# Another order of token tiles and of loads in the last step of a convolution (state-space layer beside a feed-forward layer)

## The chip, the core and the metric

The kernel runs on one core of one Trainium2 chip. The core has a matrix engine (TensorE, PE in the profile), a vector engine (VectorE, DVE), a scalar engine (ScalarE, ACT), GpSimd (POOL) and SyncE (SP), which here only issues transfers. All transfers between HBM and the core's memory (SBUF) run on the core's 16 DMA engines, whichever queue issues them. TensorE writes its products to PSUM, from where VectorE or ScalarE fetch them.

The metric is the device time of one execution in microseconds (us). Lower is better.

## The reference: what is computed

```python
x = A_u                                   # 1 x 2048 tokens x 576
xn = layernorm(x)
K[d, l] = Re sum_n C[d, n] * exp(dt[d] * A[d, n] * l) * dt[d] * B[d, n]
conv = irfft(rfft(xn padded) * rfft(K padded))[:2048] + xn * Dskip
ffn = silu(xn @ w1) @ w2                  # 576 -> 4608 -> 576
out = x + conv + ffn
```

Everything is float32. The convolution over 2048 tokens is done in the frequency domain, as a chain of small matrix products. The last of them turns an intermediate `d2` (4096 x 576, in HBM) back into tokens.

## The kernel before

**Tokens.** The 2048 tokens are 16 tiles of 128, numbered j = 0 to 15. Each has a running sum of 128 x 576, started with x, to which the feed-forward part and the convolution are added.

**The feed-forward part is the main line.** `ffn` goes over `blocks`: two halves of the tokens (`half` 0: j 0 to 7, `half` 1: j 8 to 15), 9 chunks c of four 128-wide pieces of the hidden layer, and two blocks b of four token tiles. In a block (half, c, b), `up(blk, t)` makes piece t of the hidden layer (14 matmuls of 128 x 512, on TensorE, lines L291 to L293), which ScalarE turns into `gf` and `gh` and VectorE into `gl` (L299 to L301). `down(blk, jj)` multiplies by w2 for one token tile: two half-rows of 288 columns, 12 matmuls each (L316), into one of three PSUM buffers `ps2`, and VectorE adds each half to `acc[j]` (L320). The order in a block is one up of the next block, four downs, then three ups of the next block (`u0, d0, d1, d2, d3, u1, u2, u3`). Each is a step; there are 288 steps (`2 * NCH * 2 * (FT + 4)`). Block (1,7,0) has steps 261 to 268, (1,7,1) has 269 to 276, (1,8,0) has 277 to 284 and the last, (1,8,1), 285 to 288.

The weights of a chunk are loaded and split into a high and a low part while the previous chunk runs. `load_w1(…, t)` brings two pieces of w1 in three transfers (L246 to L248; 512, 64 and 64 KB) into `w1r`, `split_w1` makes `w1h` on ScalarE (L259) and `w1l` on VectorE (L261) for each. `load_w2` and `split_w2` do it for one piece of w2 (L269, 288 KB; L278 and L280). For the last chunk all loads are traced behind step 261, the split of the second `w1r` pair behind step 269, with the table `after` of L379. The second `w1r` pair and the last two `w2r` tiles of that chunk lie in the pool `yp`, which takes over the memory of the frequency-domain stage.

**The convolution is the side line.** `side` is a generator that yields due times, as shares of the 288 steps; `weave` (L32) runs it on whenever its due time has been reached. At its end comes `tail`, the last convolution step for tiles 0 to 7, whose sums were put away in HBM (`dr0`) after half 0.

- `conv_load(j)` (L776) brings `ys`, the 256 rows of `d2` for tile j, in two transfers of 288 KB from SyncE's queue (L780). There are `AHEAD + 2` = 8 buffers.
- `add_conv(j, dst)` (L783) is the product: 8 small matmuls on TensorE (16 in the profile, L793) into two of the three PSUM buffers `pss`, and two adds on VectorE into `dst` (L799). Its first matmul stands behind the last matmul of the feed-forward part that was traced before it.
- `load_r0(j)` (L735) brings the sums of tiles j and j + 1 back, 576 KB.
- `store` (L172) writes a finished pair of tiles, for tiles 0 to 7 from GpSimd's queue.

`tail` places its loads 0.0045 apart from 0.895 on, that is from step 258: `ys0`, `r0` 0, `ys1`, `ys2`, `r0` 2, `ys3`, `ys4`, `r0` 4, `ys5`, `ys6`, `r0` 6, `ys7`. The products of tiles 0 to 7 (`last`) have their due times 0.005 apart from 0.922 on: behind steps 266, 267, 269, 270, 272, 273, 275 and 276. With product j of tiles 2 to 7 goes the load of tile j + 6. The products of tiles 8 to 15 stand in `down` in the last chunk (L307), ahead of that tile's matmuls, with the loads of tiles 14 and 15. `d2` must be complete before the first `ys` load, because every tile needs rows of all 32 frequency steps.

**How the order on the chip comes about.** Before the program runs, a planner turns the traced instructions into one fixed queue for each engine (`schedule_with_timeline_sim`, L940): by its own timeline it gives an instruction its place when its operands are there; of several that are ready, what was traced earlier goes first, and what is traced under `tc.high_priority()` (L298, L319) before that. `behind(ins)` holds instructions behind `ins` in its queue. On the chip each engine runs its queue in that order and waits where an operand is late. SyncE's queue works the same way; each of its transfers also waits for the one eight before it to land.

Of the kernel before, what the change touches and what calls it, by code (L numbers as in the profile page):

```python
# [11 lines left out]
F32 = mybir.dt.float32  # L12
# [6 lines left out]
P = 128  # L19
# [4 lines left out]
NJ = 16  # L24
NKT = 4
HD = D // 2
# [16 lines left out]
def kernel(  # L43
# [89 lines left out]
    pins = {}  # L133

    def behind(ins):
        return tc.issue_after(ins) if ins is not None else nullcontext()
# [24 lines left out]
    def load_x(j, pool, tag, engines):  # L161

        t = pool.tile([P, 2, D], F32, tag=tag, name=f"{tag}{j}")
        for ps, v, eng in quarters(xv, engines):
            eng.dma_start(t[ps], v[:, j:j + 2])
        pairs[j] = t
        return t[:, 0, :], t[:, 1, :]

    def store(t, j, engines):

        for ps, v, eng in quarters(ov, engines):
            eng.dma_start(v[:, j:j + 2] if len(t.shape) > 2 else v[:, j], t[ps])  # L172
# [26 lines left out]
    def phase0(p0, js):  # L199
        j0 = js[0]  # L200
        xs = load_x(j0, accp, "acc", (nc.sync, nc.scalar) if j0 < 4 else (nc.sync,))
        acc.update(zip(js, xs))
        if j0:
            normed(p0, js, xs)
        else:
            for j, xj in zip(js, xs):
                normed(p0, (j,), (xj,))
# [23 lines left out]
    def ffn():  # L231
# [71 lines left out]
        def down(blk, jj):  # L303
            half, c, b = blk
            j = 8 * half + 4 * b + jj
            js = slice(jj * P, (jj + 1) * P)
            if half == 1 and c == NCH - 1:  # L307
                conv_load(j + AHEAD)
                add_conv(j, acc[j])
            for h in range(2):  # L310
                hs = slice(h * HD, (h + 1) * HD)
                po = ps2.tile([P, 512], F32, tag="ps2", name="po")
                n = 0
                for t in range(FT):
                    for g, w in ((0, 0), (0, 1), (1, 0)):
                        pins["pe"] = nc.tensor.matmul(po[:, :HD], G[blk, t][g][:, js], W2[half, c, t][w][:, hs],  # L316
                                                      start=n == 0, stop=n == 3 * FT - 1).ins
                        n += 1
                with tc.high_priority():  # L319
                    nc.vector.tensor_add(acc[j][:, hs], po[:, :HD], acc[j][:, hs])  # L320
            if half == 0 and c == NCH - 1:
                rows = slice(j * P, (j + 1) * P)
                nc.sync.dma_start(dr0[rows, :], acc[j])
                if j % 2:
                    acc[7 + j], acc[8 + j] = load_x(7 + j, accp, "acc", (nc.sync,))
# [398 lines left out]
            nc.gpsimd.dma_start(d2.rearrange("(p k) d -> k p d", k=32)[k], yo)  # L724
            yield 1 + (k + 1) / 32

    AHEAD = 6

    def tail():

        r0s = {}

        def load_r0(j):
            r0s[j] = yp.tile([P, 2, D], F32, tag="r0", name="r0", bufs=4)
            nc.sync.dma_start(r0s[j], dr0[j * P:(j + 2) * P, :].rearrange("(i p) d -> p i d", p=P))  # L735

        def last(j):
            conv_load(j + AHEAD, 8)
            add_conv(j, r0s[j - j % 2][:, j % 2, :])
            if j % 2:  # L740
                store(r0s[j - 1], j - 1, (nc.gpsimd,))

        steps, at = [], tail_at[0]
        for j in range(8):
            for f in (conv_load, load_r0)[:2 - j % 2]:
                steps.append((at, f, j))
                at += tail_at[1]
        steps += [(tail_at[2] + j * tail_at[3], last, j) for j in range(8)]
        for at, f, j in sorted(steps, key=lambda v: v[0]):
            yield at  # L750
            with behind(pins["load"]):
                f(j)

    yss = {}

# [17 lines left out]
                nc.tensor.matmul(dst, st, mv[:, hs], start=n == 0, stop=n == 3 * len(terms) - 1)  # L773
                n += 1

    def conv_load(j, first=0):  # L776
        if first <= j < NJ:
            yss[j] = yp.tile([P, 4, HD], F32, tag="ys", name="ys", bufs=AHEAD + 2)
            for h in range(2):
                nc.sync.dma_start(yss[j][64 * h:64 * h + 64],  # L780
                                  d2[j * 256:(j + 1) * 256, h * HD:(h + 1) * HD].rearrange("(q r) d -> r q d", q=4))

    def add_conv(j, dst):  # L783

        ys = yss.pop(j)
        py = [pss.tile([P, 512], F32, tag="pss", name="py") for _ in range(2)]
        first = pins["pe"]
        for n in range(8):
            q1, q2, h = n // 4, n // 2 % 2, 1 - n % 2
            o = 64 * q1 + 32 * q2  # L790
            rows = slice(64 * h, 64 * h + 64)
            with tc.high_priority() if n else nullcontext(), behind(first):
                mm = nc.tensor.matmul(py[h][o:o + 32, :HD], s4[rows], ys[rows, 2 * q2 + q1],  # L793
                                      start=True, stop=True, tile_position=(64 * h, o), skip_group_check=True)
            if n == 0:
                first = mm.ins
        for h in range(2):
            hs = slice(h * HD, (h + 1) * HD)
            nc.vector.tensor_add(dst[:, hs], py[h][:, :HD], dst[:, hs])  # L799

    def gate_of(i):

        return (FT + i * 2 * FT + 1) / (2 * NCH * 2 * 2 * FT)

    def side():
        nonlocal s4, kl, yp, pa, tail_at
        marks = (0.13, 0.597, 0.823)
        tail_at = (0.895, 0.0045, 0.922, 0.005)
        with tc.tile_pool(name="pa", bufs=4) as pa:
            for js in ((0, 1), (2, 3), (4, 5), (6, 7)):  # L810
                with behind(pins["xt3"] if js[0] > 2 else None):
                    phase0(pa, js)
                pins[f"xt{js[1]}"], pins[f"xt{js[1]}s"] = pins["xt_v"], pins["xt_s"]
                if js[0] == 2:
                    yield 0
            yield 0
        with tc.tile_pool(name="kf", bufs=1) as kfp:
            for n in ("f", "phi"):
                kf[n] = kfp.tile([P, D], F32, name=n + "T")
            with tc.tile_pool(name="nat", bufs=1) as nat, tc.tile_pool(name="pb", bufs=1) as pb:  # L820
                nt = natural(nat)
                def late(j):

                    xs = load_x(j, pb, "xj", (nc.sync,))
                    yield
                    with behind(pins["gl"]):
                        normed(pb, (j, j + 1), xs)
                    yield

                tiles = chain.from_iterable(late(j) for j in range(8, NJ, 2))  # L830
                for at, todo in ((0.0, nt), (0.0, tiles), (0.004, tiles), (0.005, tiles), (gate_of(0), nt), (0.026, tiles), (0.028, tiles), (0.036, tiles), (0.038, tiles), (gate_of(1), nt), (0.06, tiles), (gate_of(2), nt), (0.09, nt)):
                    yield at
                    with behind(pins["gl"] if at else None):
                        next(todo, None)
            with behind(pins["sd"]):
                nc.gpsimd.dma_start(f1, cf1)
            nc.sync.dma_start(vt, cv)
            with tc.tile_pool(name="up", bufs=1) as up:
                sp = spread(up)
                for n, at in enumerate(kgen()):  # L840
                    if n > 1:
                        next(sp, None)
                    yield marks[0] + at * (marks[1] - marks[0])
                for _ in sp:
                    pass
        s4p = ctx.enter_context(tc.tile_pool(name="s4p", bufs=1))
        s4 = s4p.tile([P, 32], F32, name="s4")
        nc.gpsimd.dma_start(s4, cs4)

        with tc.tile_pool(name="kl", bufs=2) as kl:  # L850
            for at in spectral():
                yield marks[1] + (at - 1) * (marks[2] - marks[1])
        yp = ctx.enter_context(tc.tile_pool(name="yp", bufs=3))
        yield from tail()

    sd = side()
    next(sd)
    fg = ffn()
# [85 lines left out]
```

## Time and profile before

| | us |
|---|---|
| three runs | 1133.81, 1135.52, 1135.73 (median 1135.52) |
| the profiled execution | 1134.37 |
| its span, first to last instruction | 1132.6 |
| mean granted TensorE clock | 0.997 |
| TensorE from 1030 to 1050, 1050 to 1070, 1070 to 1090: busy | 17.77, 17.92, 18.54 of 20 each |
| TensorE from 1090 to 1120: busy | 30.00 of 30 |
| transfers from 1029 to 1094 | 15.48 MB, 238 GB/s |
| end of the last matmul | 1128.3 |

In a profile page PE is TensorE's matmuls and PEld its weight loads; L316 is line 316 of the kernel, and `po<-w2h,gh` names the tile that is written and those that are read. `x16` counts instructions merged in a line of the timeline: first the start, then the time from first to last of them, and in brackets how long the engine had been idle and who ended that. A row of the waits gives the total in us, how many times, and the longest. A row of the table by stretches has the stretch, its length, the busy time of each engine with the number of instructions (PE, PEld, DVE, ACT, POOL), the granted clock, the share of the 16 DMA engines that was busy (sums above 1 occur, since packets overlap) and GB/s.

### The profile page before, as it was taken

What the parts mean: (1) busy time and instruction counts of PE and PEld (TensorE: products, weight loads), DVE (VectorE), ACT (ScalarE), POOL (GpSimd) and SP (SyncE); (2) the same over time, 40 slices, a digit from 0 to 9 for tenths busy, and PEclk for the clock granted to TensorE, in tenths of its full rate; (3) what the DMA queues carried; (4) which work ended last, traced back from release to release, by engine and by line L of the source; (5) the groups of instructions that cost most, each with busy time, mean ns of one, the idle gap of its engine ahead of it and who ended that gap; (6) DMA issues with size and microseconds to landing.
All of it is one profiled execution on the core that took longest, in us unless ns stands there. A gap on an engine that the chain in (4) does not pass through costs nothing.

```text
span 1132.6 us, 22870 instructions
## 1 busy us (share of the span) xinstructions
PE 1108.6 (98%) x9144; PEld 998.8 (88%) x9144; DVE 916.8 (81%) x1545; ACT 709.3 (63%) x1229; POOL 73.0 (6%) x130
## 2 busy tenths in 40 slices
PE   6999999999999999999999999999999999999898
PEld 5988889898898898889989999999999999997776
DVE  6798799999999899999999737777778787773433
ACT  4565366677767676676766636787777787772211
POOL 1100100000000000011000000000000000001110
PEclk9999999999999999999999999999999999999999
DMA  9546431425252415265743263554555454426971
GB/s 277 152 121 168 122 83 60 107 81 128 71 116 84 115 60 129 70 152 168 193 143 93 67 165 115 150 154 134 160 152 159 127 158 141 132 89 170 248 179 56
DMA packets 174971, 148.56 MB, mean 131 GB/s; under 512 B 110944, under 2 KB 141680, under 8 KB 174736
## 3 DMA queue, kind: packets, MB, share of 16 engines
q1 hardware_dynamic: 164768, 112.07, 37.8%
q0 software_dynamic: 9712, 34.14, 9.4%
q8 instruction: 72, 1.18, 0.5%
q10 hardware_dynamic: 384, 0.89, 0.3%
q14 instruction: 35, 0.29, 0.1%
HBM read 102.53 MB, written 44.61 MB: 130 GB/s over the span
## 4 chain that ended last, share of the span: by engine, by line
PE 77%; DMA 7%; DVE 7%; issue 4%; SPq 2%; ACT 2%; POOL 0%; ACTq 0%; DVEq 0%; POOLq 0%
PE po L316 33%; PE ph L291 27%; DMA ys<-d 3%; PE kp L641 3%; PE ph L293 2%; PE ph L292 2%; PE pu L773 2%; PE pk L773 2%; PE pb L773 2%; PE z L656 2%; PE pu L154 1%; SPq L228 1%; DVE st L181 1%; DMA xj<-in_A_u_dram 1%; DVE gl L301 1%
## 5 line engine op out<-in xcount | busy, mean ns | idle before, releaser
L316 PE MATMUL po<-w2h,gh 128*128 128x288 f32 x1152 | 338.6, 298 | 1.0 <-ACT w2h L278 0.9
L316 PE MATMUL po<-w2l,gh 128*128 128x288 f32 x1152 | 339.0, 295 | 0.0
L316 PE MATMUL po<-w2h,gl 128*128 128x288 f32 x1152 | 337.1, 296 | 2.0 <-DVE gl L301 1.8
L316 PEld LDWEIGHTS po<-w2h,gh 128*128 128x128 f32 x1152 | 215.9, 188 | 11.6 <-issue 3.7
L316 PEld LDWEIGHTS po<-w2h,gl 128*128 128x128 f32 x1152 | 216.1, 188 | 4.8 <-DVE gl L301 2.8
L316 PEld LDWEIGHTS po<-w2l,gh 128*128 128x128 f32 x1152 | 217.0, 188 | 3.7
L299 ACT ACTIVATE gf<-ph 128x512 f32<-128x512 f32 (+1 forms) x148 | 86.5, 585 | 126.1 <-PE ph L293 109.3
L320 DVE TENSOR_TENSOR acc<-po,acc 128x288 f32<-128x288 f32 x288 | 127.1, 454 | 46.9 <-PE po L316 45.0
L291 PE MATMUL ph<-xh,w1h 128*128 128x512 f32 (+1 forms) x592 | 163.3, 391 | 1.4 <-ACT xh L124 0.7
L291 PE MATMUL ph<-xl,w1h 128*128 128x512 f32 (+1 forms) x592 | 162.9, 389 | 0.0
L291 PE MATMUL ph<-xh,w1l 128*128 128x512 f32 (+1 forms) x592 | 162.5, 387 | 0.3 <-DVE w1l L261 0.3
L301 DVE TENSOR_TENSOR gl<-gf,gh 128x512 fp32r<-128x512 f32 (+1 forms) x148 | 99.4, 674 | 39.8 <-ACT gh L300 39.0
L291 PEld LDWEIGHTS ph<-xl,w1h 128*128 128x128 f32 x592 | 109.5, 191 | 20.7
L291 PEld LDWEIGHTS ph<-xh,w1l 128*128 128x128 f32 x592 | 108.2, 189 | 21.0 <-DVE w1l L261 0.7
L291 PEld LDWEIGHTS ph<-xh,w1h 128*128 128x128 f32 x592 | 105.7, 190 | 20.3 <-issue 2.3
L300 ACT CAST gh<-gf 128x512 fp32r<-128x512 f32 (+1 forms) x148 | 89.8, 609 | 14.2 <-PE po L316 11.2
L278 ACT CAST w2h<-w2r 128x576 fp32r<-128x576 f32 x72 | 46.9, 672 | 44.8 <-PE po L316 27.9
L600 ACT ACTIVATE c<-th 128x1040 f32<-128x1040 f32 x36 | 38.7, 1074 | 49.3 <-DVE th L599 49.3
L598 ACT ACTIVATE c<-th,magic 128x1040 f32<-128x1040 f32 x36 | 42.0, 1168 | 33.2 <-DVE th L584 17.2
L261 DVE TENSOR_TENSOR w1l<-w1r,w1h 128x640 fp32r<-128x640 f32 x72 | 57.1, 822 | 0.2
L292 PE MATMUL ph<-x,w1h 128*128 128x512 f32 (+1 forms) x148 | 57.1, 386 | 0.0
L293 PE MATMUL ph<-x,w1l 128*128 128x512 f32 (+1 forms) x148 | 57.1, 386 | 0.0
(182 smaller groups left out, 1829.2 us busy)
## 6 DMA issues: line engine op xcount, KB each, us to landing
w2r<-in_B_w_dram SPq DMA_DIRECT2D x72, 288.0 KB, 3.3
w1r<-in_B_w_dram SPq DMA_DIRECT2D x35, 512.0 KB, 4.1
d1u<-u POOLq DMA_DIRECT2D x32, 288.0 KB, 2.7
d1k<-stage SPq DMA_DIRECT2D x18, 512.0 KB, 7.4
ur<-d1u SPq DMA_DIRECT2D x32, 288.0 KB, 4.1
kr<-d1k SPq DMA_DIRECT2D x32, 288.0 KB, 2.8
d<-yo POOLq DMA_DIRECT2D x32, 288.0 KB, 3.6
ys<-d SPq DMA_DIRECT2D x32, 288.0 KB, 12.4
```

The costliest lines, as they stand in the source:

```text
L261: pins["w1l"] = nc.vector.tensor_sub(l1, src, h1).ins
L278: pins["w2h"] = nc.scalar.copy(h2, r2).ins
L291: nc.tensor.matmul(ph, w[:, kt, :], v[:, kt, a:e], start=n + kt == 0, stop=False)
L292: nc.tensor.matmul(ph, h1[:, 4, :], x4[:, a:e], start=False, stop=False)
L293: pins["pe"] = nc.tensor.matmul(ph, l1[:, 4, :], x4[:, a:e], start=False, stop=True).ins
L299: nc.scalar.activation(gf, ph, AF.Silu)
L300: pins["gh"] = nc.scalar.copy(gh, gf).ins
L301: pins["gl"] = nc.vector.tensor_sub(gl, gf, gh).ins
L316: pins["pe"] = nc.tensor.matmul(po[:, :HD], G[blk, t][g][:, js], W2[half, c, t][w][:, hs], start=n == 0, stop=n == 3 * FT - 1).ins
L320: nc.vector.tensor_add(acc[j][:, hs], po[:, :HD], acc[j][:, hs])
L598: nc.scalar.activation(c65, th, AF.Identity, bias=magic)
L773: nc.tensor.matmul(dst, st, mv[:, hs], start=n == 0, stop=n == 3 * len(terms) - 1)
```

## The change

The product order becomes 0 to 3, 8 to 11, 4 to 7, 12 to 15, and the loads follow the same order through one iterator. The first eight `ys` loads and two of the `r0` loads are traced together at 0.897, step 259, ahead of the weights of the last chunk (step 261). Each product, after its own matmuls and adds, calls for the next load. Products 0 to 3 have due times that put them behind steps 269 to 272, products 4 to 7 behind 278, 279, 280 and 282; `r0` 4 and `r0` 6 are loaded after products 1 and 2. The products of tiles 8 to 15 stay in `down`, so that in block (1,8,0) the order on TensorE is to be 8, down 0, 4, 9, down 1, 5, 10, down 2, 6, 11, down 3, an up, 7. The number of buffers stays 8.

```diff
             if half == 1 and c == NCH - 1:
-                conv_load(j + AHEAD)
                 add_conv(j, acc[j])
+                conv_load()
...
-    AHEAD = 6
+
+    order = iter((0, 1, 2, 3, 8, 9, 10, 11, 4, 5, 6, 7, 12, 13, 14, 15))
...
         def last(j):
-            conv_load(j + AHEAD, 8)
             add_conv(j, r0s[j - j % 2][:, j % 2, :])
+            conv_load()
             if j % 2:
                 store(r0s[j - 1], j - 1, (nc.gpsimd,))
 
-        steps, at = [], tail_at[0]
+        yield tail_at[0]
+        with behind(pins["load"]):
+            for j in (0, None, 2, None, None, None, None, None):
+                conv_load()
+                if j is not None:
+                    load_r0(j)
         for j in range(8):
-            for f in (conv_load, load_r0)[:2 - j % 2]:
-                steps.append((at, f, j))
-                at += tail_at[1]
-        steps += [(tail_at[2] + j * tail_at[3], last, j) for j in range(8)]
-        for at, f, j in sorted(steps, key=lambda v: v[0]):
-            yield at
-            with behind(pins["load"]):
-                f(j)
+            if j in (2, 3):
+                load_r0(j * 2)
+            yield tail_at[1 + j // 4] + j % 4 * tail_at[3]
+            last(j)
...
-    def conv_load(j, first=0):
-        if first <= j < NJ:
-            yss[j] = yp.tile([P, 4, HD], F32, tag="ys", name="ys", bufs=AHEAD + 2)
+    def conv_load():
+
+        j = next(order, None)
+        if j is not None:
+            yss[j] = yp.tile([P, 4, HD], F32, tag="ys", name="ys", bufs=8)
...
-        tail_at = (0.895, 0.0045, 0.922, 0.005)
+        tail_at = (0.897, 0.932, 0.965, 0.0036)
```

## The prediction

> **What bounds the kernel now.** I read the page first, then the waits, then the timelines of TensorE, of SyncE's queue and of VectorE over the last 110 us. The page:
>
> ```profile
> PE 1108.6 (98%) x9144; PEld 998.8 (88%) x9144; DVE 916.8 (81%) x1545; ACT 709.3 (63%) x1229; POOL 73.0 (6%) x130
> ys<-d SPq DMA_DIRECT2D x32, 288.0 KB, 12.4
> ```
>
> TensorE is busy for 98% of the span, so a change can win only where it idles. A `ys` half takes 12.4 us from issue to landing; a lone load of 288 KB takes 2.8 us (`kr<-d1k`, 288.0 KB, 2.8, on the same list): transfers queue up. The waits of TensorE from 1020 us to the end are one line, and its timeline shows where:
>
> ```profile
> PE py L793 <- DMA ys<-d: 5.8, 4, 2.1
> ```
>
> ```profile
> 1036.91 0.71 PE L793 MATMUL py<-ys,s 64*32 64x288 f32 x16
> ...
> 1039.97 0.69 PE L793 MATMUL py<-ys,s 64*32 64x288 f32 x8 [0.99 <-DMA ys<-d]
> ...
> 1048.90 0.84 PE L793 MATMUL py<-ys,s 64*32 64x288 f32 x16 [1.23 <-DMA ys<-d]
> ...
> 1055.18 0.84 PE L793 MATMUL py<-ys,s 64*32 64x288 f32 x16 [2.08 <-DMA ys<-d]
> ...
> 1056.46 0.44 PE L316 MATMUL po<-w2h,gh 128*128 128x288 f32 x1
> ```
>
> Products 1, 2, 3 and 7 wait for their `ys` tile, 5.8 us together. After the longest gap 14 matmuls run at a pace of 0.24 us instead of 0.13 (0.44 us each instead of 0.29). SyncE's queue shows in which order the transfers stand, and the table by stretches what the DMA engines can do:
>
> ```profile
> 1029.41 1.28 SPq L780 DMA_DIRECT2D ys<-d  x2
> 1030.74 0.60 SPq L735 DMA_DIRECT2D r<-dr  x1
> 1031.38 1.24 SPq L780 DMA_DIRECT2D ys<-d  x2
> 1032.66 0.61 SPq L246 DMA_DIRECT2D w1r<-in_B_w_dram  x1
> ...
> 1034.38 0.60 SPq L248 DMA_DIRECT2D w1r<-in_B_w_dram  x1
> 1035.02 1.06 SPq L269 DMA_DIRECT2D w2r<-in_B_w_dram  x2
> 1037.52 1.59 SPq L780 DMA_DIRECT2D ys<-d  x2
> ```
>
> ```profile
> 1029.40:1046.30 16.90, 15.90 (x102) 11.77 (x101) 6.34 (x12) 4.91 (x8) 1.16 (x3) 1.00 0.97 226
> 1046.30:1061.00 14.70, 11.39 (x88) 9.71 (x88) 5.74 (x13) 3.04 (x5) 2.74 (x6) 0.88 1.07 253
> ```
>
> The last two columns are the DMA engines' busy share and GB/s: from 1029.4 us, when the last write of `d2` has landed (issue 1026.79, 2.4 us), they are full at 226 to 253 GB/s. It is one pipe, emptied in SyncE's order. The `w1r` block of three transfers is the second pair of w1 chunks of the very last FFN step; today it stands behind two `ys` tiles and one `r0` and has landed at 1043.0 (1034.4 + 8.7).
>
> **What the change takes away.** Products 0 and 1 now come after the up-projection that ends at 1047.66, and product 4 follows 8. Sixteen products remain, with the same matmuls, adds and stores; they cost nothing more.
> Without products 0 and 1 before it TensorE gets to the first one at 1036.91 + 0.69 (three matmuls left of that up at 0.23) + 2 x 3.20 (an up: 1101.71 to 1104.91) = 1044.0. Products alternating with downs follow each 4.02 us (1085.70, 1089.71, 1093.74, 1097.77): products 1, 2, 3 at 1048.0, 1052.1, 1056.1. Their data: `ys0` landed at 1034.7 (1030.1 + 4.6), `ys1` at 1039.9; the next unit of 576 KB adds some 2.4 us (576 KB at 240 GB/s, between the two rates), so `ys2`, `r0` 2 and `ys3` land near 1042, 1045 and 1048. All four are early: -5.77 us (0.99 + 1.23 + 2.08 + 1.46). With the 2.08 us gap goes the slow stretch: 14 x 0.11 = -1.53.
> A product's group costs 4.02 - 24 x 0.131 = 0.88 us. Products 1 and 7 are split into two groups of 8 today (1039.97 and 1043.33; 1080.85 and 1082.13): -1.76 if they stay whole. In return 9, 10 and 11 now come directly behind 4, 5 and 6, each taking two of three `pss` buffers: the second half of each must wait for VectorE's add and will be split. That is +2.64 for three, between -0.6 (none split, three transitions of about 0.2 saved) and +3.5 (four).
> Later loads: `ys4` and its followers stand behind the weights, six `ys` and two `r0` or 4.6 MB less what is needed first; at 240 GB/s `ys4` lands near 1069, `ys7` near 1083. They are needed from 1077 and from 1094. Tiles 12 to 15 are triggered from about 1073 on and needed from 1101: 2.4 MB or 10 us, hidden by block (1,8,0). If that cover fell away, each would cost up to 2.4.
> So far: -5.77 - 1.53 - 1.76 + 2.64 = **-6.4 us**.
>
> **What the change adds.** The ten loads of the first batch are traced at step 259, ahead of the last weights at 261. Today only `ys0`, `r0` 0 and `ys1` are. So `ys2`, `r0` 2, `ys3` and `ys8` to `ys11` step in front of that `w1r` block: 7 x 576 KB = 4.13 MB, 16.3 to 18.3 us at the two rates. It lands at 1043.0 + 17.3 = 1060.3, and with part of the store of tokens 0 and 1 in the pipe at about 1061 (1060 to 1063).
> TensorE needs it only for the third up of block (1,8,0), at 1060.1 + 3.2 = 1063.3; ScalarE's split takes 1.35 for two chunks (1048.85), so that alone fits. But the split's second half, `w1l` (L261), is an instruction in VectorE's queue, and a queue runs in the planner's order:
>
> ```profile
> 1051.82 0.82 DVE L799 TENSOR_TENSOR r<-py,r 128x288 f32<-128x288 f32 x2 [5.36 <-DMA r<-dr]
> 1052.56 0.68 DVE L301 TENSOR_TENSOR gl<-gf,gh 128x512 fp32r<-128x512 f32 x1
> 1053.16 1.55 DVE L261 TENSOR_TENSOR w1l<-w1r,w1h 128x640 fp32r<-128x640 f32 x2
> 1054.63 0.45 DVE L320 TENSOR_TENSOR acc<-po,acc 128x288 f32<-128x288 f32 x1
> ```
>
> Here `gl`, whose `gh` was ready at 1048.95, sits 3.6 us behind an add that waits for `r0` 2: the planner had believed that load earlier than the chip delivers. How much earlier can be read from TensorE's order. The planner put product 1 at most 2.1 us behind product 0 (1036.91, and 1039.97 less the gap of 0.99), with three transfers of 1152 KB between their landings; the chip took 5.3 (1034.6 to 1039.9). From `ys0` to the end of the `w1r` block there are now 19 transfers or 5824 KB. Planned by number that is 13 us, by size 10.5: the planner sees the block between 1047 and 1050, the chip at 1061. ScalarE's half comes first (0.67), so `w1l` is queued in VectorE somewhere between 1048 and 1051, amid the adds of downs 0 and 1 of block (1,7,1).
> Behind it wait L320, which frees the three `ps2` buffers, and L799, which frees `pss`. TensorE can run three half-downs past the first held add. `w1l` is through at 1061 + 0.67 + 0.67 + 0.8 = 1063.2, the first held add at 1063.7. If that is the second half of down 0, TensorE stops at 1052.8 and loses 10.9; first half of down 1: 1054.4, 9.3; second half: product 3 stops at 1056.4 and loses 7.3. Bounds: placed right behind `gl`, as now, it stops at 1050.3 (13.4); placed behind the adds of down 2, nothing. I take 9, the middle one. After such a stop comes a slow stretch like the one at 1056.46: +1.5.
> Sum: -6.4 + 9 + 1.5 = +4.1.
>
> On that 1.5: the Trainium skill, page "TensorE: Matmul & The Clock Gate", Part 1, has TensorE fall to half clock after an idle window of about 3.4 us. The 2.08 us gap here already did it, at a granted clock of 0.88 over that stretch, so the trace is harsher; by the rule the gaps taken away would give back 5.77 alone, and the sum would be 1.5 higher.
>
> **Rivals.** *The weights are in time or the split is queued late: faster.* For it: TensorE itself needs them only at 1063.3, and the adds of L320 are traced with high priority, the split is not. Against it: the planner's order above. Without the 9 and the 1.5 the sum is -6.4: about 1128 (1125 to 1130 with the groups).
> Beside this stands a page's figure. The Trainium skill, "DMA: Bandwidth & Descriptors", Specifications, gives a core about 358 GB/s from HBM; at that rate the block would land near 1055 and the hold shrink to 3 or 4 us. No stretch here reaches it for long (226 to 253), so I give it 3% of the 12% below.
> *A short hold.* `w1l` is queued behind product 2's adds, and TensorE stops only in down 3, for 4 to 6 us: -6.4 + 5 + 1.5 = 0, so 1134 to 1136.
> *The hold is longer.* As now right behind `gl`: -6.4 + 13.4 + 1.5 = +8.5, 1143 to 1145. This is the forecast's far end.
> *The triggers starve the queue.* A late product would delay the next load. Against it: the backlog on SyncE lasts to about 1083, beyond all triggers but the last two, which have 20 us. I give it no chance of its own.
>
> **How the numbers follow.** The profiled execution took 1134.37 us (span 1132.6, and 1.8 around it); the three runs have a median of 1135.52 and go from 1133.81 to 1135.73, so it lies inside, 1.15 under the median. 1134.4 + 4.1 = 1138.5; half of that distance added, **1139 us**. Within 0.2% (2.3 us, about what a measurement of this kernel can tell from no change) counts as the same.
> The hold of 7 us or more: 58%. The short one: 12%, of which 8 same, 2 faster, 2 slower. In time: 30%. So faster 0.32, same 0.08, slower 0.60. The forecast's own range is 1136 to 1145; with the faster case taken in, **1127 to 1145**.
>
> **What would show it.** SyncE's queue: ten loads (18 transfers) in a row from 1029.4, then `w1r`. TensorE's waits: no line `py <- DMA ys`; in its place a wait of `po` or `py` for VectorE's L320 or L799 near 1053 to 1064. VectorE: one idle stretch of 8 to 13 us before L261, put down to `w1h` or `w1r`. Wrong: `w1r` issued before `ys2`; L261 behind the adds of down 2; or `ys` waits that remain.

## The result, and the profile after

| | before | after |
|---|---|---|
| median of 21 runs each (lowest to highest) | 1133.66 us (1128.34 to 1138.24) | 1136.54 us (1133.68 to 1141.66) |
| ratio, 95% interval | | 1.0027 (1.0014 to 1.0039) |
| span of the profiled execution | 1132.6 | 1134.2 |
| mean granted clock | 0.997 | 0.995 |
| issue of the last write of `d2` (L724) | 1026.79 | 1024.31 |
| from there to the end of the span | 105.8 | 109.9 |

The change costs 0.27%, or 2.9 us between the medians. The first 1024 us run the same work in both kernels and still differ by 2.5 us between the two profiled executions, so the spans compare badly. The last row leaves that out. It is the measure used below: the tail, from the issue of the last `d2` write to the end. By it the change costs 109.9 - 105.8 = **4.1 us**.

The page of the kernel after, with the engines' busy time and the DMA issues of `ys` (count, KB each, median us from issue to landing):

```profile
PE 1107.7 (98%) x9144; PEld 996.7 (88%) x9144; DVE 917.0 (81%) x1545; ACT 710.2 (63%) x1229; POOL 73.0 (6%) x130
...
ys<-d SPq DMA_DIRECT2D x32, 288.0 KB, 9.9
```

Nothing was added to TensorE's work, and a `ys` half lands sooner after its issue, 9.9 us for 12.4. The gain aimed at is there. The waits of TensorE from 1020 us on (total, how often, longest) have again one line, another one:

```profile
PE po L316 <- DVE acc L320: 8.0, 1, 8.0
```

No product waits for `ys` any more; one down waits for VectorE. TensorE's timeline at that place:

```profile
1051.22 0.71 PE L797 MATMUL py<-ys,s 64*32 64x288 f32 x16
...
1053.42 0.29 PE L316 MATMUL po<-w2h,gl 128*128 128x288 f32 x1
1061.71 0.61 PE L316 MATMUL po<-w2h,gh 128*128 128x288 f32 x1 [8.00 <-DVE acc L320]
1062.12 0.44 PE L316 MATMUL po<-w2l,gh 128*128 128x288 f32 x1
...
1064.89 1.21 PE L797 MATMUL py<-ys,s 64*32 64x288 f32 x16
```

TensorE stands still for 8.00 us in the middle of down 2, and then each matmul shows 0.44 us instead of 0.29 and a product 1.21 instead of 0.71. SyncE's queue tells where it began:

```profile
1026.91 1.28 SPq L784 DMA_DIRECT2D ys<-d  x2
...
1032.57 14.39 SPq L784 DMA_DIRECT2D ys<-d  x10
1047.68 0.38 SPq L246 DMA_DIRECT2D w1r<-in_B_w_dram  x1
1048.97 0.50 SPq L247 DMA_DIRECT2D w1r<-in_B_w_dram  x1
1050.27 0.48 SPq L248 DMA_DIRECT2D w1r<-in_B_w_dram  x1
```

Eighteen transfers, sixteen `ys` halves and two `r0`, stand in a row, and the first of the `w1r` block is issued 20.8 us after the first `ys` (1047.68 - 1026.91); before it was 3.3 (1032.66 - 1029.41). Each of the block's issues comes some 1.3 us behind the other, since each waits for an older transfer to land. The chain of waits (start, us, what) takes it from there:

```profile
1037.29 12.96 DMA ys<-d
...
1050.27 9.27 DMA w1r<-in_B_w_dram
...
1059.71 0.73 ACT w1h L259
...
1060.47 0.66 DVE w1l L261
...
1061.21 0.46 DVE acc L320
...
1061.71 3.25 PE po L316 x12
```

The issue of the last `w1r` transfer waits until a `ys` half has landed; the transfer lands at 1059.54; ScalarE splits off `w1h`, VectorE `w1l`; only then comes the add that frees a `ps2` buffer. VectorE's timeline shows that the add had no need of any of this:

```profile
1047.72 0.46 DVE L803 TENSOR_TENSOR r<-py,r 128x288 f32<-128x288 f32 x1 [0.75 <-PE py L797]
1060.47 0.83 DVE L261 TENSOR_TENSOR w1l<-w1r,w1h 128x640 fp32r<-128x640 f32 x1 [12.29 <-ACT w1h L259]
1061.21 0.45 DVE L320 TENSOR_TENSOR acc<-po,acc 128x288 f32<-128x288 f32 x1
1061.58 0.81 DVE L261 TENSOR_TENSOR w1l<-w1r,w1h 128x640 fp32r<-128x640 f32 x1
1062.31 0.45 DVE L320 TENSOR_TENSOR acc<-po,acc 128x288 f32<-128x288 f32 x1
```

The split stands right behind product 1's two adds and holds VectorE for 12.29 us. TensorE fills the three `ps2` buffers meanwhile and then stops. The table by stretches (length; busy us and count of PE, PEld, DVE, ACT, POOL; granted clock; DMA share; GB/s) on both sides of the restart:

```profile
1053.71:1061.71 8.00, 0.00 (x1) 0.00 (x0) 1.24 (x3) 1.35 (x2) 0.00 (x0) 0.67 1.06 373
1061.71:1066.67 4.96, 4.96 (x30) 3.76 (x31) 3.07 (x8) 0.00 (x0) 0.00 (x0) 0.50 1.08 204
```

From the restart 4.96 us run at a granted clock of 0.50. In that time (1061.71 to 1066.68) ran 12 matmuls, a product and two matmuls more. At full clock they would take 2.68 us: 11 times the pace of 0.131, and the 1.24 us that the same sequence around product 2 took (1051.00 to 1052.24). So some 2.3 us are lost besides the 8.0.

### The profile page after: what moved, and what is told of

It reads as the page before. It is cut to its first block, busy times and chain, and to the rows that moved or that the text cites. A ratio compares the mean times of both kernels' runs of the same rounds, so it can differ in the third digit from the quotient of the medians.

```text
span 1134.2 us, 22869 instructions
## 1 busy us (share of the span) xinstructions
PE 1107.7 (98%) x9144; PEld 996.7 (88%) x9144; DVE 917.0 (81%) x1545; ACT 710.2 (63%) x1229; POOL 73.0 (6%) x130
## 4 chain that ended last, share of the span: by engine, by line
PE 65%; DVE 18%; DMA 7%; issue 6%; ACT 3%; SPq 1%; POOL 0%; DVEq 0%; ACTq 0%; POOLq 0%
PE po L316 28%; PE ph L291 23%; PE pu L775 2%; PE pk L775 2%; PE pb L775 2%; PE ph L293 2%; PE ph L292 2%; DVE acc L320 2%; DMA ys<-d 2%; PE kp L641 2%; DMA w2r<-in_B_w_dram 2%; DMA w1r<-in_B_w_dram 2%; DVE th L582 2%; DVE gl L301 1%; DVE S L620 1%
## 5 line engine op out<-in xcount | busy, mean ns | idle before, releaser
L316 PE MATMUL po<-w2h,gh 128*128 128x288 f32 x1152 | 339.1, 298 | 9.5 <-DVE acc L320 8.2
L316 PE MATMUL po<-w2h,gl 128*128 128x288 f32 x1152 | 337.4, 296 | 2.3 <-DVE gl L301 2.3
L316 PE MATMUL po<-w2l,gh 128*128 128x288 f32 x1152 | 339.0, 295 | 0.2 <-DVE w2l L280 0.2
L316 PEld LDWEIGHTS po<-w2h,gh 128*128 128x128 f32 x1152 | 215.7, 188 | 23.0 <-DVE acc L320 9.9
L316 PEld LDWEIGHTS po<-w2h,gl 128*128 128x128 f32 x1152 | 216.0, 188 | 7.0 <-DVE gl L301 3.1
L316 PEld LDWEIGHTS po<-w2l,gh 128*128 128x128 f32 x1152 | 216.8, 188 | 4.3 <-DVE w2l L280 0.4
L320 DVE TENSOR_TENSOR acc<-po,acc 128x288 f32<-128x288 f32 x288 | 126.4, 451 | 37.4 <-PE po L316 35.1
L259 ACT CAST w1h<-w1r 128x640 fp32r<-128x640 f32 x72 | 48.7, 724 | 15.1 <-DMA w1r<-in_B_w_dram 14.8
```

The source lines that it names most:

```text
L259: nc.scalar.copy(h1, src)
```

## The experiments

The theory: the `w1r` block lands late because it stands in SyncE's queue behind the whole batch, and this costs time because `w1l` stands in VectorE's queue ahead of adds that could go. The rivals: the late block itself holds TensorE, wherever the split is queued; the new product order costs time by itself; the pipe has no room, so that the block would be late from any queue. Every kernel below was timed in five rounds beside the kernel before on the same chip. "Groups" are the stretches of product matmuls on TensorE from 1020 us to the end, counted in its timeline (19 in the kernel before, 21 after).

| kernel | median us (before beside it) | ratio, 95% interval | tail, against 105.8 | groups |
|---|---|---|---|---|
| weights first | 1128.05 (1133.33) | 0.9955 (0.9938 to 0.9971) | 100.2, -5.6 | 22 |
| split queued later | 1126.37 (1133.33) | 0.9943 (0.9924 to 0.9963) | 99.4, -6.4 | 21 |
| batch alone, old order | 1139.27 (1133.33) | 1.0056 (1.0035 to 1.0076) | 113.2, +7.4 | 19 |
| weights first, products 4 to 7 spread | 1126.19 (1133.33) | 0.9947 (0.9927 to 0.9967) | 99.5, -6.3 | 21 |
| old order, weights first | 1126.00 (1135.12) | 0.9930 (0.9912 to 0.9948) | 99.5, -6.3 | 21 |
| weights from GpSimd's queue | 1128.64 (1135.12) | 0.9947 (0.9928 to 0.9966) | 100.6, -5.2 | 22 |

**Weights first.** The kernel after, with the batch due behind step 261, where the weights are traced, and not at 259:

```diff
-        tail_at = (0.897, 0.932, 0.965, 0.0036)
+        tail_at = (0.908, 0.932, 0.965, 0.0036)
```

> The changed kernel with one number altered: the batch of ten loads is due at 0.908 (step 262) instead of 0.897, so it stands behind the last weights in SyncE's queue. Theory (the late w1r block holds VectorE's queue, and with it TensorE): w1r lands some 15 us earlier, the 12.3 us idle stretch of VectorE before L261 and the 8.0 us stop of TensorE before L316 are gone, and so is the half clock of 10.2 us that followed; ys0 lands some 5 us later than in the changed kernel and still ahead of product 0. Time 6 us under the kernel before (5 to 8), 9 to 11 under the changed one. Rival (the split product groups cost the time, ten groups for seven products in block (1,8,0)): those groups stay, so the time stays within 1 us of the changed kernel.

The block now stands ahead of the batch. First SyncE's queue, then VectorE's timeline of this kernel:

```profile
1027.74 0.38 SPq L246 DMA_DIRECT2D w1r<-in_B_w_dram  x1
...
1030.46 1.28 SPq L784 DMA_DIRECT2D ys<-d  x2
```

```profile
1045.91 0.45 DVE L320 TENSOR_TENSOR acc<-po,acc 128x288 f32<-128x288 f32 x1
1046.28 1.55 DVE L261 TENSOR_TENSOR w1l<-w1r,w1h 128x640 fp32r<-128x640 f32 x2
1047.74 0.45 DVE L320 TENSOR_TENSOR acc<-po,acc 128x288 f32<-128x288 f32 x1
```

`w1l` stands even earlier among the adds than in the kernel after, between the two of down 0, and takes its 1.55 us without a wait. TensorE has no wait at all from 1020 us on, and no stretch at half clock there. A single number of the due times makes 9.7 us of the tail (109.9 - 100.2).

**Split queued later.** The kernel after with its late block, and only the place of the split changed: it is traced at down 3 instead of the first up of block (1,7,1), and VectorE's half is held behind the latest add of L320:

```diff
-                with behind(pins["xt1"] if first else None):
+                with behind(pins["xt1"] if first else pins["add"] if half == 1 and c == NCH - 1 and t else None):
...
-                    nc.vector.tensor_add(acc[j][:, hs], po[:, :HD], acc[j][:, hs])
+                    pins["add"] = nc.vector.tensor_add(acc[j][:, hs], po[:, :HD], acc[j][:, hs]).ins
...
-                    (1, "u0"): [(split_w1, 2), (split_w2, 0)],
-                    (1, "d3"): [(split_w2, 1), (split_w2, 2)],
+                    (1, "u0"): [(split_w2, 0)],
+                    (1, "d3"): [(split_w1, 2), (split_w2, 1), (split_w2, 2)],
```

> The changed kernel with the late loads left as they are, but the w1l half of the last split is put behind VectorE's last add of down 3 of block (1,7,1). Theory (it is the place in VectorE's queue that costs, not the late landing): w1r still lands near 1059, VectorE goes on with the adds, TensorE does not stop in downs 1 to 3, and the time is 9 to 11 us under the changed kernel, some 6 under the kernel before; at most 1 us of waiting for w1l before the third up. Rival (TensorE needs the weights themselves): TensorE then stops at the third up of block (1,8,0) for several us and the time falls by under 4.

ScalarE's and VectorE's timelines of this kernel:

```profile
1061.55 1.35 ACT L259 CAST w1h<-w1r 128x640 fp32r<-128x640 f32 x2 [14.83 <-DMA w1r<-in_B_w_dram]
```

```profile
1064.18 0.45 DVE L320 TENSOR_TENSOR acc<-po,acc 128x288 f32<-128x288 f32 x1
1064.55 1.55 DVE L261 TENSOR_TENSOR w1l<-w1r,w1h 128x640 fp32r<-128x640 f32 x2
```

The block is as late as in the kernel after: it lands at 1061.37, 9.28 us after an issue at 1052.09, and ScalarE waits 14.83 us for it. TensorE has no wait, and the tail is the shortest of all, 99.4. So a landing 32 us after the first `ys` issue costs nothing; what costs is the adds that stand behind the split. The first rival falls.

**Batch alone.** The kernel before, its product order and all, with its loads 0.0008 apart instead of 0.0045, so that all twelve units are traced ahead of the weights:

```diff
-        tail_at = (0.895, 0.0045, 0.922, 0.005)
+        tail_at = (0.895, 0.0008, 0.922, 0.005)
```

> The kernel before, product order 0 to 15 and old due times, but its twelve loads of tiles 0 to 7 are all traced ahead of the last weights (spacing 0.0008 instead of 0.0045). Theory (loads ahead of the weights cost the time): nine units of 576 KB now stand ahead of w1r, it lands near 1065 instead of 1043, VectorE is held before L261 and TensorE stops for 10 to 14 us in block (1,7,1), half clock behind it; waits of products 2, 3 and 7 (4.8 us) and their slow stretch (1.5) vanish. Time 4 to 10 us over the kernel before. Rival (the new product order costs the time): the order is the old one here, so the time falls by 4 to 6 us with the waits.

VectorE's and TensorE's timelines, and the stretch after the restart:

```profile
1054.17 0.46 DVE L320 TENSOR_TENSOR acc<-po,acc 128x288 f32<-128x288 f32 x1 [0.91 <-PE po L316]
1070.13 1.56 DVE L261 TENSOR_TENSOR w1l<-w1r,w1h 128x640 fp32r<-128x640 f32 x2 [15.50 <-ACT w1h L259]
1071.61 1.18 DVE L320 TENSOR_TENSOR acc<-po,acc 128x288 f32<-128x288 f32 x3
```

```profile
1072.11 0.61 PE L316 MATMUL po<-w2h,gh 128*128 128x288 f32 x1 [12.55 <-DVE acc L320]
```

```profile
1072.10:1077.00 4.90, 4.89 (x20) 4.89 (x21) 2.06 (x6) 0.84 (x2) 0.00 (x0) 0.50 1.09 228
```

The same hold, longer, under the old product order: 15.50 us on VectorE, 12.55 on TensorE, again about 5 us at half clock. The new order is not needed for the loss; that rival falls. The three kernels also give a scale. From the first `ys` issue to the landing of the block it takes 13.6 us with three units ahead (before), 32.6 with ten (after) and 38.9 with twelve (here): 2.7 to 2.8 us for each unit of 576 KB more than in the kernel before.

**Products 4 to 7 spread.** Weights first, and the due times of products 4 to 7 later, so that each would stand apart from its neighbour and need not be split:

```diff
-        tail_at = (0.908, 0.932, 0.965, 0.0036)
+        tail_at = (0.908, 0.932, 0.9755, 0.0034)
```

> As the first of these runs (weights ahead of the batch), and products 4 to 7 are due behind steps 281 to 284, between the ups of block (1,8,0), instead of directly beside products 9 to 11. Theory (a group of py costs 0.88 us whatever its length, and neighbours split because pss has three buffers): block (1,8,0) has 8 to 10 groups for eight products instead of 11, and the time is 1 to 3 us under the first run, 7 to 9 under the kernel before. Rival (splits are hidden): no difference to the first run beyond 0.5 us.

A miss in size: the tail is 0.7 us shorter than with the weights first alone, not 1 to 3. Only one group of 22 went, because the planner split other products in the place of those. The intervals of the two kernels overlap, so even the 0.7 rests on single profiles. It fits the rest, though: the tails with 21 groups are 99.4, 99.5 and 99.5, those with 22 are 100.2 and 100.6.

**Old order, weights first.** The kernel before, its order of tiles kept, all its loads together behind the weights and its products 0 to 7 due from step 269 on, where the change puts product 0:

```diff
-        tail_at = (0.895, 0.0045, 0.922, 0.005)
+        tail_at = (0.908, 0.00005, 0.932, 0.0036)
```

> The kernel before with its product order 0 to 15 and its triggers, but the twelve loads of tiles 0 to 7 stand behind the last weights (due at 0.908) and products 0 to 7 are due behind steps 269 to 276. Theory (the gain comes from meeting the transfers later, not from the new order of tiles): w1r first in SyncE's queue, ys0 some 5 us later, ys7 near 1065, product 7 due on TensorE near 1071; no waits of TensorE for ys or for VectorE; 5 to 7 us under the kernel before, as the run with the weights first. Rival (the new order is needed to spread the transfers): waits for ys of 3 us or more come back at products 4 to 7, and the time is at most 3 us under the kernel before.

It is as fast as the best with the new order: 0.9930 beside 0.9943 and 0.9947, with intervals that overlap widely. TensorE has no wait from 1020 us on here either. So the new order of the tiles brings nothing that due times don't bring. Which of the two due times does how much was not tried.

**Weights from GpSimd's queue.** The kernel after, the three transfers of the block issued by GpSimd:

```diff
-            eng = nc.gpsimd if first and t == 0 else nc.sync
+            eng = nc.gpsimd if first and t == 0 or last and t else nc.sync
```

> The changed kernel, with the three transfers of that last w1r block issued from GpSimd's queue instead of SyncE's; the batch still stands ahead of everything else in SyncE's queue. Theory (the block is late because it stands in line behind 18 transfers, not because the engines have no share left for it): it is issued as soon as its memory is free and lands 7 to 10 us later, as the stores from GpSimd do beside a full SyncE queue (7.6 us before); no hold, 5 to 7 us under the kernel before, 8 to 10 under the changed one. Rival (the DMA engines serve in the order of all issues): it lands some 20 us or more after issue and the hold stays above 4 us.

GpSimd's queue of this kernel, and the start of SyncE's:

```profile
1029.14 0.77 POOL L246 DMA_DIRECT2D w1r<-in_B_w_dram  x1 [3.03 <-DVE acc L320]
```

```profile
1028.17 1.28 SPq L784 DMA_DIRECT2D ys<-d  x2
1029.50 0.60 SPq L736 DMA_DIRECT2D r<-dr  x1
1030.14 3.19 SPq L784 DMA_DIRECT2D ys<-d  x4
```

The block lands between 1036.6 and 1038.2, 7.4 to 7.8 us after its issues, and TensorE doesn't wait. So it need not be late beside the batch. What made it late was its place in SyncE's queue: in the kernel after its first transfer is issued only at 1047.68, and the hold goes when it is issued early from another queue. How the DMA engines share between two queues this run doesn't show, and the rival of the expectation, service in the order of all issues, is not excluded: when GpSimd issued the last transfer of the block, at 1030.42, SyncE had issued only four of its eighteen. Those 1440 KB and the block's 640 KB, one after the other at the prediction's 240 GB/s, would be through some 9 us after 1028.17, near 1037 by this estimate, and that is about what was measured. The Trainium skill, page "DMA: Bandwidth & Descriptors", section "Issuing engines are not separate DMA queues", says that another issuing engine saves only the time of issuing, since all transfers share the 16 DMA engines. The pair of runs says more: from the other queue the block landed 22.6 us earlier, counted in each run from the issue of the last `d2` write, mostly because its first transfer was issued 19.8 us earlier, counted the same way.

## Why the prediction was right

**Mechanism and place.** SyncE's order, the late block, the split in VectorE's queue amid the adds, the stop in L316 for L320: each came as forecast. The three experiments on the block (moved ahead, split moved behind, other queue) each took the hold away and left -5.2 to -6.4 us in the tail. That is near the -6.4 which the prediction worked out for its faster rival and for the part that the change takes away.

**The landing.** Forecast near 1061 (1060 to 1063) in the clock of the kernel before; measured 1059.54, and 2.48 more in that clock, or 1062.0. Seven units more took 32.6 - 13.6 = 19.0 us, where 16.3 to 18.3 were reckoned.

**The size of the hold: 9, measured 8.0.** The first held add was that of down 1's first half, the middle one of the three cases, priced at 9.3. In the clock of the kernel before TensorE stopped at 1053.71 + 2.48 = 1056.2, 1.8 later than that case had it, and went on at 1064.2, 0.5 later. Four matmuls of the next up (0.92 us from 1048.61 on) stood in between, which the forecast had not there; that product 1 came in two groups took up most of the rest (0.77, below). The short hold (4 to 6) and the long one (13.4) fell for this kernel; batch alone shows that 12.55 is possible.

**The half clock: 1.5, measured 2.3.** A mis-sized term. I took over the loss from before, where one window was slow; a stop of 8 us left 4.96 us slow after it. The last section shows where such stretches began and ended.

**The groups: +0.88 net, measured two groups more.** Product 7 stayed whole as forecast, product 1 did not. In block (1,8,0) seven products came in ten groups, three more, as forecast. The first of them on TensorE's timeline of the kernel after:

```profile
1082.97 0.72 PE L797 MATMUL py<-ys,s 64*32 64x288 f32 x16
1085.80 0.69 PE L797 MATMUL py<-ys,s 64*32 64x288 f32 x8
1087.01 0.72 PE L797 MATMUL py<-ys,s 64*32 64x288 f32 x16
1089.03 0.69 PE L797 MATMUL py<-ys,s 64*32 64x288 f32 x8
```

A row of 8 is half a product; the x16 between two such rows is two halves of neighbours. What a split costs can be read around product 1. In two groups it sets the matmuls of the downs back by 1.62 us: 2.41 from the one at 1045.54 to the sixth after it at 1047.95, less six times 0.131. Product 2 in one group sets them back by 0.85: 1.24 from 1051.00 to the third after it at 1052.24, less three times 0.131. So the second group adds 0.77 us, a little under the 0.88 of the forecast, and the tails with 21 and with 22 groups differ by 0.7 to 1.2.

**The sum.** +4.1 forecast, +4.1 measured, and that is closer than its terms, so in part luck: with the sizes measured above it is -5.77 - 1.53 + 8.0 + 2.3 + 2 x 0.77 = +4.5. The hold was 1.0 shorter than forecast, the half clock cost 0.8 more, the groups 0.7 more, and 0.4 too much is left. It is no accident of one profile: without hold and half clock the same sum, with each kernel's own groups, is too high by 0.2 to 0.6 in all five experiments that have no stop (weights first: -7.3 + 3 x 0.77 = -5.0, measured -5.6). The table by stretches over each whole tail shows that the waits are not to blame. TensorE is idle there for 10.10 us before and 12.37 after, 2.27 more, which is what the waits say (8.00 - 5.77 = 2.23). It is busy for 95.71 us before and 97.52 after, 1.81 more, where the terms of the half clock and the groups make 2.3. Which of its work got shorter stays open.

**The time.** 1139 was worked out from three runs and a profiled execution near 1135; the median of before is 1133.66 over 21 runs, which range over 10 us. The difference was forecast at 4.1 and is 1.6 to 4.4 by the interval (0.14% to 0.39% of 1133.66).

## What to carry to other kernels

Before you put a batch of loads ahead of others in one queue, look for the smallest load that it passes and for the engine that must touch that load next: an instruction that waits there holds everything behind it in its engine's queue, needed or not. Two remedies are equally good here within their intervals: trace the small load first, or queue its consumer behind the work that doesn't need it. And count a long stop dearer than its length: after both stops here, of 8.00 and 12.55 us, TensorE ran at half clock for some 5 us more.

## What the runs showed of the hardware that was not expected

In the kernel before a gap of 2.08 us brought half clock and one of 1.46 did not. In these two profiles the granted clock changes only at steps 3.413 us apart, and cutting the trace at these steps orders the cases. The table by stretches, first of the kernel before:

```profile
121.17:124.59 3.42, 1.85 (x11) 1.44 (x11) 3.42 (x8) 3.15 (x6) 0.84 (x2) 1.00 0.33 122
124.59:128.00 3.41, 3.41 (x11) 2.74 (x10) 3.41 (x6) 1.77 (x4) 0.00 (x0) 0.50 0.44 110
1053.01:1056.43 3.42, 1.34 (x20) 0.81 (x20) 3.42 (x7) 0.00 (x0) 0.00 (x0) 1.00 1.06 300
1056.43:1059.84 3.41, 3.41 (x17) 3.41 (x16) 0.94 (x3) 0.00 (x0) 1.93 (x4) 0.50 1.10 207
1076.91:1080.33 3.42, 2.47 (x11) 1.69 (x9) 1.24 (x2) 1.16 (x3) 0.00 (x0) 1.00 1.04 336
1080.33:1083.74 3.41, 2.90 (x22) 1.50 (x23) 1.51 (x3) 0.34 (x1) 0.11 (x1) 1.00 1.09 223
```

and of the kernel after:

```profile
121.17:124.59 3.42, 1.96 (x11) 1.53 (x11) 3.42 (x6) 3.42 (x6) 0.00 (x0) 1.00 0.49 192
124.59:128.00 3.41, 3.41 (x22) 3.07 (x21) 3.41 (x7) 0.85 (x2) 0.00 (x0) 1.00 0.51 76
...
1059.84:1063.25 3.41, 1.53 (x6) 1.54 (x7) 2.78 (x6) 1.22 (x2) 0.00 (x0) 0.50 1.07 280
1063.25:1066.67 3.42, 3.42 (x26) 2.23 (x25) 1.53 (x5) 0.00 (x0) 0.00 (x0) 0.50 1.09 213
1066.67:1070.08 3.41, 3.41 (x26) 3.32 (x26) 1.57 (x4) 1.25 (x2) 1.93 (x4) 1.00 1.08 227
```

Read them in pairs: the idle time of a window (length less PE's busy time) and the clock of the next. 1.57 and 2.08 idle: the next at 0.50. 1.46 and 0.95 idle: the next at full clock. The gap of 1.46 us at 1079.39 lies on both sides of a step and falls to 0.95 and 0.51. After the 8 us stop the window in which work resumed was still idle for 1.88 of 3.41, and so the next one, fully busy, ran at half. In these two profiles, between 20 and 1120 us, no window with up to 1.46 us idle was followed by a lower clock, and each with 1.57 or more was. A threshold it is not: in the kernel after, the window from 1128.11 us, in which the last matmul ends, was idle for 1.69 us and the next one stayed at full clock, and so it was after 1.87 us idle in the window from 1119.89 of the run with the weights from GpSimd's queue. In batch alone a window at half clock with 1.42 us idle (from 1070.69) was followed by another at half clock. What decides beside the idle time stays open. Still, a stop can cost more than its length, here 2.3 us more after 8.00 and 1.5 us more after 2.08, and where it falls on the grid counts. The Trainium skill, page "TensorE: Matmul & The Clock Gate", Part 1, has a free-running window of 3413 ns, which agrees with these steps, and a fall to half clock after a window of idleness; here 1.57 us of idle time in one was enough.
